# Gated mix of attention and a squared-ReLU MLP: the second chunk's q and k by seven block products

## The chip, the cores and the metric

The kernel runs on one core of a Trainium2 chip. The metric is the device time of one execution in microseconds. Beside it stands one execution that the hardware profiler recorded; every start and duration below is from that recording, counted from the start of its span.

## The reference, cut to what matters

2048 tokens of width 448 go through two branches that a gate mixes, all in fp32:

```python
qkv = x @ wqkv                      # 448 -> 3 x 448, 16 heads of 28
logits = q . k at offsets 0, 2, .., 14 back (8 keys), scaled, masked
a = (softmax(logits) @ v) @ wo
h = relu(x @ w1 + b1) ** 2          # 448 -> 1792
b = h @ w2 + b2
g = sigmoid((x * gate_w).sum(-1))
out = g * a + (1 - g) * b
```

## The kernel before

**Arithmetic.** Each fp32 operand of a matmul is cut into a high and a low part (`split_full`: ACT writes the high part at L130, DVE subtracts it at L131), and a product is made of three matmuls: high by high, high by low, low by high. PE therefore works on half arrays in pairs (`side_by_side` L194 to L202 and `beside` L349, whose matmuls are issued by `Bank.add` at L344): one product goes through the upper 64 rows of the array while another goes through the lower 64. The trace lists the two of a pair as single instructions.

**Stages.** The tokens are worked in four chunks of 512. First come q, k and v of chunk 0 (`qkv_first`), of chunk 1 (two calls of `qkv_two`, each for 256 tokens), of chunk 2 (`qkv_seven`) and of chunk 3 (`qkv_two` twice, with the first groups h of the MLP between). `qkv_seven` does q and k of two token halves by Strassen's way: seven block products (banks x, y, z, w and so on in the trace, numbered 1 to 7 in the code) in place of eight, from sums of token blocks (`token_sums`) and sums of weight blocks (`weight_sums`), which DVE makes and `split_full` cuts. Its v goes through the class `V`, without sums. After that comes the MLP, chunk by chunk (h, then b = h @ w2), and at the end a @ wo (the banks a and last). Attention runs beside this in 8 units (`par`, `g`): a unit loads q, k and v (L532, L533, L538) from DRAM, POOL multiplies (L561, L568) and DVE reduces (L562, L576).

**Where q, k and v go.** A finished PSUM bank is copied by ACT into an SBUF tile (`qkv_evacuate` L243, in `qkv_seven` `copied` L433 and `added` L437 on DVE) and stored to DRAM by SP (`stage_store` L235, into q_d, k_d and v_d). These tiles, named st in the trace, come from the pool tag "stage", which has three buffers (`ST_BUFS`) used in turn: a fourth tile can be written only when the first one's store has landed. `qkv_seven` takes the stage tile of its second token half from another tag ("e5"), and chunk 2's v goes to the tag "pp" and to two tiles of other use (`own_v`, `b2t`). A bank that PE will go on with after its copy is "turned" first (a memset of one element by DVE, L212 and L360), and the copy itself must be done before PE writes the bank again.

**Order of the work.** PE's order is that of the code. Everything else is placed by a planner's clock, in ns: `advance` adds 203 for each pair of matmuls that PE is given, and `when(t, ...)`, `steps(t, gap, ...)` and `at(dt, ...)` emit their work as the clock passes t. The trace runs 5.7 to 5.9 us behind this clock. So each engine's list, SP's DMA list too, is fixed in the program, and each engine takes its list in order: an instruction that waits holds up all behind it. The numbers that matter here are those of `SPLIT_AT` (cuts of chunk c of x, from raw tiles into the tiles x), the spill of x to DRAM (`x_spill`, L157, four stores of 512 KB into x_d for each chunk), the loads and cuts of w1 in four pieces (`w1_piece`, load at L759), and the load of w2 (`w2_piece`, load at L792 into the tile w2raw, whose four rows are cut by `split_copied`: ACT writes the high part at L745 and a copy into PSUM at L746, DVE the low part at L751).

## Time and profile before

| | us |
|---|---|
| median of 3 runs (lowest, highest) | 413.1 (412.44, 413.24) |
| the profiled execution's own time | 412.9 |
| its span | 411.1 |
| PE busy | 406.5 |
| DVE, ACT, POOL busy | 278.8, 218.0, 267.8 |
| mean granted clock of PE | 1.0 |

The span is what the core's instructions cover; the 1.8 us between it and the execution's time lie outside the program's instructions. Busy time of PE counts a matmul from its start to its modelled end, and a share near 100% means that PE had nearly always something in flight. Names in the trace drop the numbers of buffers: `st<-qkv` is a copy of some qkv bank into some stage tile.

### The profile page before, as it was taken

The numbers are of one execution on the slowest core, as the hardware profiler recorded it, in microseconds if no ns is written. First come the engines' busy times: TensorE is split into PE (matmuls) and PEld (weight loads), VectorE is DVE, ScalarE is ACT, GpSimd is POOL, SyncE is SP. The second block draws the span as 40 slices with busy tenths as digits, with TensorE's granted clock in tenths as the row PEclk, the third lists the DMA queues.
The fourth block names the chain that finished last, engine by engine and source line by source line (L and its number), as shares of the span: only waits on it lengthen the run. The fifth ranks groups of instructions, "written<-read, shape, count | busy, mean of one in ns | idle before, by whom it ended". The sixth has DMA issues, their size and how long they took to land.

```text
span 411.1 us, 9365 instructions
## 1 busy us (share of the span) xinstructions
PE 406.5 (99%) x3817; PEld 398.4 (97%) x3817; DVE 278.8 (68%) x454; ACT 218.0 (53%) x494; POOL 267.8 (65%) x167
## 2 busy tenths in 40 slices
PE   8999999999999999999999999999999999999997
PEld 7999999999999999999999999999999999999996
DVE  4575866484868667587665888788676776784344
ACT  5664777474875455445565435454653254356640
POOL 0000000966999999989898899899899797950000
PEclk9999999999999999999999999999999999999999
DMA  7999899989271514554113638875146530058404
GB/s 231 347 353 341 247 365 299 367 233 334 97 262 76 208 36 151 206 186 153 19 68 120 206 100 239 238 190 162 38 145 202 216 130 0 25 153 156 119 2 180
DMA packets 67020, 74.00 MB, mean 180 GB/s; under 512 B 33504, under 2 KB 59296, under 8 KB 66848
## 3 DMA queue, kind: packets, MB, share of 16 engines
q1 hardware_dynamic: 66976, 73.39, 56.2%
q8 instruction: 30, 0.49, 0.5%
q14 instruction: 14, 0.11, 0.1%
HBM read 45.94 MB, written 28.25 MB: 180 GB/s over the span
## 4 chain that ended last, share of the span: by engine, by line
PE 98%; DMA 1%; DVE 0%; SPq 0%; issue 0%
PE b L202 33%; PE h L202 32%; PE qkv L202 17%; PE a L202 7%; PE v L344 2%; PE qkv L291 2%; PE x L344 1%; PE z L344 1%; PE a L1273 1%; DMA xraw<-xT 1%; PE y L344 1%; PE w L344 1%; PE last L1273 0%; DVE bt L1152 0%; SPq L886 0%; PE last L1265 0%
## 5 line engine op out<-in xcount | busy, mean ns | idle before, releaser
L561 POOL TENSOR_TENSOR qk<-q,k 128x896 f32<-128x896 f32 x64 | 134.9, 2143 | 82.2 <-DMA k<-k_d 76.8
L568 POOL TENSOR_TENSOR av<-lg,v 128x896 f32<-128x896 f32 x64 | 119.2, 1970 | 5.0 <-DVE lg L562 4.8
L866 DVE TENSOR_TENSOR h<-h,h 128x512 fp32r<-128x512 f32 x56 | 38.5, 687 | 60.2 <-ACT h L869 60.1
L202 PE MATMUL b<-w2ah,h 64*128 64x448 f32 x448 | 71.9, 359 | 0.0
L202 PE MATMUL b<-w2bh,h 64*128 64x448 f32 x448 | 71.6, 359 | 0.0
L576 DVE TENSOR_REDUCE o<-av 128x112 f32<-128x896 f32 x64 | 66.6, 1070 | 0.5 <-POOL av L568 0.3
L562 DVE TENSOR_REDUCE lg<-qk 128x32 f32<-128x896 f32 x64 | 66.9, 1074 | 0.0
L867 ACT ACTIVATE h<-h,b1z 128x512 f32<-128x512 f32 x56 | 36.7, 655 | 42.4 <-PE h L202 42.4
L202 PE MATMUL qkv<-wqh,x 64*128 64x448 f32 (+1 forms) x384 | 57.4, 360 | 0.0
L202 PEld LDWEIGHTS b<-w2ah,h 64*128 64x128 f32 x448 | 50.8, 184 | 0.0
L202 PEld LDWEIGHTS b<-w2bh,h 64*128 64x128 f32 x448 | 50.5, 184 | 0.0
L202 PE MATMUL b<-w2al,h 64*128 64x448 f32 x224 | 46.8, 358 | 0.0
L202 PE MATMUL b<-w2bl,h 64*128 64x448 f32 x224 | 46.7, 358 | 0.0
L202 PEld LDWEIGHTS qkv<-wqh,x 64*128 64x128 f32 x384 | 36.5, 184 | 2.5
L202 PE MATMUL qkv<-wql,x 64*128 64x448 f32 (+1 forms) x192 | 35.2, 360 | 0.0
L868 ACT ACTIVATE h<-h 128x512 fp32r<-128x512 f32 x56 | 33.6, 599 | 1.7
L869 ACT ACTIVATE h<-h 128x512 f32<-128x512 f32 x56 | 33.2, 594 | 0.0
L814 ACT ACTIVATE h<-h 128x4 fp32r<-128x4 f32 (+1 forms) x35 | 7.2, 207 | 44.0 <-PE b L202 41.6
L202 PEld LDWEIGHTS b<-w2al,h 64*128 64x128 f32 x224 | 27.3, 184 | 0.0
L202 PEld LDWEIGHTS b<-w2bl,h 64*128 64x128 f32 x224 | 27.1, 184 | 0.0
L243 ACT ACTIVATE st<-qkv 128x448 f32<-128x448 f32 x36 | 18.1, 542 | 16.3 <-PE qkv L202 13.8
L202 PEld LDWEIGHTS qkv<-wql,x 64*128 64x128 f32 x192 | 18.4, 184 | 1.3
(263 smaller groups left out, 889.3 us busy)
## 6 DMA issues: line engine op xcount, KB each, us to landing
k<-k_d SPq DMA_DIRECT2D x8, 840.0 KB, 6.5
v<-v_d SPq DMA_DIRECT2D x8, 840.0 KB, 4.9
x_d<-x SPq DMA_DIRECT2D x12, 512.0 KB, 6.7
q_d<-st SPq DMA_DIRECT2D x8, 448.0 KB, 5.6
k_d<-st SPq DMA_DIRECT2D x8, 448.0 KB, 5.3
w1raw<-w SPq DMA_DIRECT2D x4, 896.0 KB, 10.2
q<-q_d SPq DMA_DIRECT2D x8, 448.0 KB, 3.7
o_d<-o SPq DMA_DIRECT2D x16, 224.0 KB, 2.3
```

The lines of the kernel that those rows point to most:

```text
L202: nc.tensor.matmul(acc.pt[:, :acc.n], a[rows], w[rows], start=acc.todo == acc.all, stop=acc.todo == 1)
L243: nc.scalar.activation(st[:, :, t % 2], heads(pt), AF.Copy)
L291: nc.tensor.matmul(acc.pt[:, :D], a, w, start=k == j == 0, stop=False)
L344: nc.tensor.matmul(self.pt[:, :self.n], a, w, start=new, stop=True, skip_group_check=True)
L561: nc.gpsimd.tensor_mul(pr, q[:, s:s + 1].to_broadcast([P, W, C]), k[:, s:s + W])
L562: pending.append(lambda: nc.vector.tensor_reduce(lg[:, s], pr.rearrange("p w (h d) -> p w h d", h=HG), axis=AX.X, op=ALU.add))
L568: nc.gpsimd.tensor_mul(pr.rearrange("p (h d) w -> p w h d", h=HG), lg[:, s][:, :, :, None].to_broadcast([P, W, HG, DH]), v[:, s:s + W].rea ...
L576: nc.vector.tensor_reduce(o[:, g * C:(g + 1) * C], pr, axis=AX.X, op=ALU.add)
L866: nc.vector.tensor_sub(hl, pt, f32(hh))
L867: ops += [lambda pt=pt, r=r: nc.scalar.activation(pt, pt, AF.Relu, bias=b1t[:, f + r:f + r + 1]), lambda pt=pt, hh=hh: nc.scalar.activatio ...
L868: lambda pt=pt, hh=hh: nc.scalar.activation(hh, pt, AF.Square),
L869: lambda pt=pt, r=r, low=low: (nc.scalar.activation(pt, pt, AF.Square), at(delays[r], low))]
```

## The change

`qkv_seven(1, ...)` takes the place of chunk 1's two `qkv_two`. Its v goes through `V` with stage tiles of the pool (`inner` is None). `token_sums(1)` is made on chip into tiles of x0, x1 and the attention's tag "v". The sums of the weights, and their cuts, are emitted from clock 8300 on instead of 17000. In the table, entries after chunk 1 move; the first load of w2 moves from 85500 to 87000 and its cuts stay at 93200, and the spill of chunk 2's x moves from 40000 to 71000. Attention's start moves by 2500.

```diff
-ATT_DELAY = 16000.0
+ATT_DELAY = 18500.0
...
             a, b = sums[self.c, (None, 1, 0, 0, 1)[n]], (None, 1, 0, 1, 0)[n]
-            o = (2 * self.u + b) * P if j < 2 else CH + b * P
-            return tuple(t[:, o:o + P] for t in a)
+            o = (2 * self.u + b) * P if j < 2 else b * P
+            return tuple(t[:, o:o + P] for t in a[j // 2])
...
-                if self.inner == "pp":
+                if self.inner in (None, "pp"):
                     qkv_evacuate(bank.pt, self.c, tl, 2, self.inner)
...
-    SPLIT_AT = {1: 19000.0, 2: 35000.0, 3: 53500.0}
+    SPLIT_AT = {1: 18800.0, 2: 33200.0, 3: 51700.0}
...
+        one = [lambda: sub(q0, k0, q0), lambda: sub(k0, k1, k0), lambda: sub(k1, k1, q0), lambda: sub(q1, q1, k1)]
+        two = [lambda: sub(q2, k2, q2),
+               lambda: sub(k2[LOW], o[LOW], k2[LOW]), lambda: sub(k2[HIGH], m[HIGH], k2[HIGH]),
+               lambda: sub(z[LOW], o[LOW], q2[LOW]), lambda: sub(z[HIGH], m[HIGH], q2[HIGH]),
+               lambda: sub(m[LOW], m[LOW], z[LOW]), lambda: sub(m[HIGH], o[HIGH], z[HIGH])]
+        cuts = [cut((1, False), q0), cut((3, False), k0), cut((2, False), k1), cut((4, False), q1)]
+        cuts += [lambda: split_full(o, *w7x, soon)]
+        return one, two, cuts, [cut((1, True), q2), cut((2, True), z), cut((4, True), m), cut((3, True), k2)]
...
         def begin():
+            if c == 1:
+                t = [xpool.tile([P, 2 * CH], F32R, tag=f"x{n}", name=f"s{c}_0{'hl'[n]}")[:, 48:48 + CH + 2 * P] for n in range(2)]
+                sums[c, 0] = [[v[:, :CH] for v in t], [v[:, CH:] for v in t]]
+                t = attp.tile([P, 48 + 2 * (CH + 2 * P)], F32R, tag="v", name=f"s{c}_1")[:, 48:]
+                t = [t[:, n * (CH + 2 * P):(n + 1) * (CH + 2 * P)] for n in range(2)]
+                sums[c, 1] = [[v[:, :CH] for v in t], [v[:, CH:] for v in t]]
+                return
...
-    steps(17000.0, 900.0, weight_sums())
+    one, two, cuts, more = weight_sums()
+    steps(8300.0, 700.0, one)
+    steps(13600.0, 700.0, cuts)
+    steps(16300.0, 700.0, two)
+    steps(27000.0, 0.0, more[:1])
+    steps(30500.0, 900.0, more[1:])
     for c, t in SPLIT_AT.items():
         when(t, x_begin, c)
         for k in range(4):
             when(t + k * 900.0, lambda c, k: x_split(xraw[c], xs[c], k, soon if c == 3 else now), c, k)
         if c < 3:
-            when(t + 5000.0, lambda c: x_spill(c, xs[c]), c)
+            when((0.0, 24000.0, 71000.0)[c], lambda c: x_spill(c, xs[c]), c)
     when(23500.0, x_more, 2)
     when(39500.0, x_more, 3)
 
-    def sums_begin():
-        made, cuts = token_sums(2)
-        steps(43000.0, 850.0, made)
-        steps(50300.0, 2100.0, cuts)
-    when(42500.0, sums_begin)
+    def sums_begin(c, t, gap, t_cut, gap_cut):
+        made, cuts = token_sums(c)
+        steps(t, gap, made)
+        steps(t_cut, gap_cut, cuts)
+    when(23300.0, sums_begin, 1, 23400.0, 850.0, 27500.0, 2000.0)
+    when(40900.0, sums_begin, 2, 41000.0, 850.0, 48500.0, 2100.0)
     when(10500.0, x_spill, 0, x)
-    when(25000.0, w1_piece, 0, 38000.0, 1500.0)
+    when(25000.0, w1_piece, 0, 37000.0, 1500.0)
     when(44500.0, halos)
-    when(45500.0, w1_piece, 1, 58000.0, 1300.0)
-    when(66800.0, w1_piece, 2, 76300.0, 1400.0)
-    when(67800.0, w1_piece, 3, 83500.0, 900.0)
+    when(44500.0, w1_piece, 1, 56200.0, 1300.0)
+    when(65000.0, w1_piece, 2, 74500.0, 1400.0)
+    when(66000.0, w1_piece, 3, 85000.0, 850.0)
     for j in range(2):
-        when(65500.0 + j * 2000.0, x_copy, 3, j)
-    when(78500.0, biases)
-    when(85500.0, w2_piece, 0, 4, 93200.0, 1500.0)
-    when(89100.0, w2_piece, 4, 3, 99700.0, 1400.0)
+        when(63700.0 + j * 2000.0, x_copy, 3, j)
+    when(76700.0, biases)
+    when(87000.0, w2_piece, 0, 4, 93200.0, 1500.0)
+    when(89600.0, w2_piece, 4, 3, 99700.0, 1400.0)
...
-    qkv_two(xs[1], 1, 0)
-    qkv_two(xs[1], 1, 2)
+    qkv_seven(1, xs[1], (None, None))
```

PE's chunk 1 before consists of 252 half matmuls of `side_by_side`; now it has 234 of `Bank.add`, and the rest of PE's list is as it was. In the second pass over a bank (`other`, `second`) PE waits for the ACT copy of what the first pass left there.

**ACT, the copies of chunk 1.** ACT's list before, where the first q and k banks of chunk 1 are copied into stage tiles (st1_0_0 holds q, st1_1_1 k, x2 are chunk 2's tokens):

```order
L243 ACTIVATE st1_0_0_649<-qkv1_0_0_534 128x4x112 [waits DMAHW6_49,PE_49,Activation_49]
L243 ACTIVATE st1_1_1_651<-qkv1_1_1_537 128x4x112 [waits DMAHW3_49,Activation_49]
L130 ACTIVATE tw8_208<-wqraw0_3_153 64x448 [waits DVE_49]
L130 ACTIVATE x2_0_666<-xraw2_0_487 128x512 [waits DMAHW7_49,DMAHW1_49]
L130 ACTIVATE tw8_208<-wqraw7_172 64x448 [waits DVE_49]
L130 ACTIVATE x2_1_667<-xraw2_1_488 128x512 [waits DMAHW2_49,DMAHW0_49]
L243 ACTIVATE st1_0_0_649<-qkv1_1_0_535 128x4x112 [waits PE_49]
L243 ACTIVATE st1_1_1_651<-qkv1_0_1_536 128x4x112
L130 ACTIVATE x2_2_668<-xraw2_2_489 128x512 [waits DMAHW1_49]
```

And in the change, where v, x and z are copied (st1_0_2 is v's tile of tokens 0 and 1, DMAHW is a wait on a DMA):

```order
L130 ACTIVATE tw8_208<-wqraw0_3_153 128x448
L130 ACTIVATE w2ah_74<-wqraw1_164 128x448
L433 ACTIVATE st1_0_0_660<-x1_0_584 128x4x112 [waits DVE_49,DMAHW3_49,PE_49,Activation_49]
L433 ACTIVATE st1_1_0_662<-x1_1_586 128x4x112 [waits DVE_49]
L130 ACTIVATE x2_0_673<-xraw2_0_499 128x512 [waits DMAHW7_49,DMAHW1_49]
L130 ACTIVATE x2_1_674<-xraw2_1_500 128x512 [waits DMAHW2_49,DMAHW0_49]
L130 ACTIVATE x2_2_675<-xraw2_2_501 128x512 [waits DMAHW1_49]
L130 ACTIVATE x2_3_676<-xraw2_3_502 128x512 [waits DMAHW4_49,DMAHW2_49]
L433 ACTIVATE st1_0_1_714<-z1_0_664 128x4x112 [waits DVE_49,DMAHW1_49,PE_49,Activation_49]
L433 ACTIVATE st1_1_1_716<-z1_1_666 128x4x112 [waits DMAHW2_49,DVE_49,Activation_49]
```

The cuts of x2 now stand between x's copies and z's, and each of the two z copies waits for a DMA: the first for the v_d store of st0_2_2, the second for the v_d store of st1_0_2. PE's second pass over z waits for the second of them.

**SP, behind chunk 0.** SP's list of DMAs before, from the load of the first piece of w1 (st0 are chunk 0's tiles, st1 chunk 1's):

```order
L759 DMA w1raw0_524<-w1 128x4x448 [waits DMAHW0_49]
L235 DMA v_d_59<-st0_2_2_528 128x4x224 [waits DMAHW1_49,Activation_49]
L235 DMA q_d_57<-st1_0_0_649 128x4x224 [waits DMAHW2_49,Activation_49]
L235 DMA k_d_58<-st1_1_1_651 128x4x224 [waits DMAHW3_49,Activation_49]
L235 DMA v_d_59<-st1_0_2_712 128x4x224 [waits DMAHW4_49,Activation_49]
L808 DMA xraw3_772<-xT 128x2048 [waits DMAHW5_49]
```

The same piece of SP's list in the change (halo0 are the zeros ahead of the first token):

```order
L759 DMA w1raw0_537<-w1 128x4x448 [waits DMAHW0_49]
L235 DMA v_d_59<-st0_2_2_541 128x4x224 [waits DMAHW1_49,Activation_49]
L235 DMA v_d_59<-st1_0_2_626 128x4x224 [waits DMAHW2_49,Activation_49]
L808 DMA xraw3_765<-xT 128x2048 [waits DMAHW3_49,DVE_49]
L1021 DMA k_d_58<-halo0_128 8x7x112 [waits DMAHW4_49,Pool_49]
L1021 DMA v_d_59<-halo0_128 8x7x112 [waits DMAHW5_49]
```

Now a v_d store of chunk 1 follows the v_d store of chunk 0 at once, and the q_d and k_d stores of chunk 1 come later, behind the halos and the second w1 load.

**SP, around the first w2 load.** SP's list before, from the load of the bias b2 (q01 and k01 are loads for the attention, st3 chunk 3's tiles):

```order
L1025 DMA b2t_76<-b2 128x448 [waits DMAHW5_49,DMAHW1_49]
L532 DMA q01_1430<-q_d_57 128x896 [waits DMAHW6_49,Pool_49]
L533 DMA k01_1431<-k_d_58 128x1680 [waits DMAHW7_49]
L792 DMA w2raw0_1444<-w2 128x4x448 [waits DMAHW0_49,Activation_49]
L235 DMA q_d_57<-st3_0_0_1412 128x4x224 [waits Activation_49]
L235 DMA k_d_58<-st3_1_1_1414 128x4x224 [waits DMAHW2_49,Activation_49]
L235 DMA v_d_59<-st3_0_2_1478 128x4x224 [waits DMAHW3_49,Activation_49]
L792 DMA w2raw4_1539<-w2 128x3x448 [waits DMAHW4_49,DVE_49]
```

SP's list in the change, at the same place:

```order
L1025 DMA b2t_76<-b2 128x448 [waits DMAHW5_49,DMAHW1_49]
L235 DMA q_d_57<-st3_0_0_1423 128x4x224 [waits DMAHW6_49,Activation_49]
L235 DMA k_d_58<-st3_1_1_1425 128x4x224 [waits DMAHW7_49,Activation_49]
L532 DMA q01_1472<-q_d_57 128x896 [waits DMAHW0_49,Pool_49]
L533 DMA k01_1473<-k_d_58 128x1680
L235 DMA v_d_59<-st3_0_2_1479 128x4x224 [waits DMAHW2_49,Activation_49]
L792 DMA w2raw0_1543<-w2 128x4x448 [waits DMAHW3_49]
L792 DMA w2raw4_1554<-w2 128x3x448 [waits DMAHW4_49,DVE_49]
```

The load w2raw0 stood ahead of the three stores of st3 and now stands behind them. The four x_d stores of chunk 2, which stood behind xraw3, come now between chunk 2's q_d and v_d stores.

**ACT, around the cuts of w2raw0.** In the change, where the copies of chunk 3's third q and fourth k bank stand (st3_2_0, st3_3_1):

```order
L745 ACTIVATE w2ah_74<-w2raw0_1543 128x448 [waits DMAHW3_49]
L746 ACTIVATE copy6_1491<-w2raw0_1543 128x448 [waits Activation_49]
L745 ACTIVATE w2ah_74<-w2raw0_1543 128x448
L746 ACTIVATE copy6_1491<-w2raw0_1543 128x448 [waits DVE_49]
L243 ACTIVATE st3_2_0_1615<-qkv3_2_0_1485 128x4x112 [waits DMAHW6_49,PE_49]
L243 ACTIVATE st3_3_1_1617<-qkv3_3_1_1488 128x4x112 [waits DMAHW7_49]
L745 ACTIVATE w2ah_74<-w2raw0_1543 128x448
```

Before, three pairs of cut and copy stood ahead of st3_2_0; now two pairs do. In both, PE's next h group waits for the copy into st3_2_0.

More of the change, by code (lines that the diff above doesn't have):

```diff
@@ L944, in weight_sums @@
         (q0, q1, q2, m), (k0, k1, k2) = ([t[:, :D] for t in raws[b]] for b in range(2))
-        o = raw7[:, 1, :D]
+        o, z = raw7[:, 1, :D], raw7[:, 0, :D]
         sub = nc.vector.tensor_sub
@@ L949, in cut @@
             return lambda: split_full(t, *wsum[key], soon)
[L951 to L965 removed]
+        one = [lambda: sub(q0, k0, q0), lambda: sub(k0, k1, k0), lambda: sub(k1, k1, q0), lambda: sub(q1, q1, k1)]
[6 more added lines that the diff above has]
+        return one, two, cuts, [cut((1, True), q2), cut((2, True), z), cut((4, True), m), cut((3, True), k2)]
     def token_sums(c):
[L969 removed]
+        raw = xraw[c] if isinstance(xraw[c], list) else [xraw[c][:, k, :CH] for k in range(4)]
         add, sub = nc.vector.tensor_add, nc.vector.tensor_sub
@@ L980, in begin @@
         def begin():
+            if c == 1:
[5 more added lines that the diff above has]
+                return
             for j in range(2):
-                sums[c, j] = [halfp.tile([P, FA], F32R, tag=f"e{2 * j + n}", name=f"s{c}_{j}{'hl'[n]}")[:, 48:48 + CH + 2 * P]
-                              for n in range(2)]
+                t = [halfp.tile([P, FA], F32R, tag=f"e{2 * j + n}", name=f"s{c}_{j}{'hl'[n]}")[:, 48:48 + CH + 2 * P]
+                     for n in range(2)]
+                sums[c, j] = [[v[:, :CH] for v in t], [v[:, CH:] for v in t]]
         def cut(j):
-            split_full(raw[j], *(t[:, :CH] for t in sums[c, j]), soon)
+            split_full(raw[j], *sums[c, j][0], soon)
             for u, rows in enumerate((LOW, HIGH)):
-                split_full(raw[2 + j][rows, u * 2 * P:(u + 1) * 2 * P], *(t[rows, CH:] for t in sums[c, j]), soon)
+                split_full(raw[2 + j][rows, u * 2 * P:(u + 1) * 2 * P], *(t[rows] for t in sums[c, j][1]), soon)
         return made(0) + made(2), (lambda: (begin(), cut(1)), lambda: cut(0))
```

16 lines of the change are left out of this document (removed).

## The prediction

> **What bounds the kernel.** I read the page first: span, busy shares, granted clock.
>
> ```profile
> span 411.1 us, 9365 instructions
> PE 406.5 (99%) x3817; PEld 398.4 (97%) x3817; DVE 278.8 (68%) x454; ACT 218.0 (53%) x494; POOL 267.8 (65%) x167
> PEclk9999999999999999999999999999999999999999
> ```
>
> PE works 406.5 of 411.1 us at full clock, so a change can win only by taking matmuls out, and loses whatever PE then waits. The chain that ended last gives the stages and the price of a matmul (start, length, what).
>
> ```profile
> 13.17 43.66 PE qkv L202 x432
> 56.83 2.48 PE v L344 x24
> ...
> 60.51 1.86 PE v L344 x18
> ...
> 70.18 1.20 PE z L344 x12
> ...
> 80.53 22.99 PE qkv L202 x228
> 103.52 2.84 PE h L202 x24
> ```
>
> Each row begins where the one before ends: PE never pauses here. A half-array matmul costs 43.66/432 = 0.101 us. Those 432 are chunk 0's last 180 and chunk 1's 252, so chunk 1 begins at 13.17 + 180 × 0.101 = 31.4 and takes 25.5 us. Chunk 2, already by seven products, runs from 56.83 to 80.53: 23.7 us. Of chunk 3, the first MLP group h starts at 103.52, 23.0 us after the chunk.
>
> **What is removed.** In the changed order chunk 1 has 234 half matmuls for 252; the rest of PE's order is identical. 18 × 0.101 = **−1.8 us**, and the two chunks' lengths say the same (25.5 − 23.7). That is the whole gain.
>
> **What is added beside PE.** Eight sums and their cuts go to DVE and ACT, which stand at 68% and 53%, and the weights' sums come earlier. DVE's memsets ahead of a bank's second half now come behind more work in its list; no row shows one late, so I bound them by nothing and by one such piece of work:
>
> ```profile
> 27.88 0.67 DVE L131 TENSOR_TENSOR x<-xraw,x 128x512 fp32r<-128x512 f32 x1
> ```
>
> I take nothing for them, because the wait below, later in the same chunk, swallows a delay of 0.67 us; without that wait they would count. Attention starts 2.5 us later in the planner. That costs nothing either: wo's first use waits for PE alone, not for attention's result:
>
> ```profile
> ACT oh L1222 <- PE a L202: 9.3, 4, 2.8
> ```
>
> If that cover were gone it would cost up to those 2.5 us, at the end. The remaining w1 loads and cuts mostly move 1.0 to 1.8 us earlier with PE's shorter program, so against their users they stay. The fourth w1 piece's cuts move behind chunk 3's first q and k copies:
>
> ```profile
> 90.51 1.04 ACT L130 ACTIVATE w1bh<-w1raw 128x448 fp32r<-128x448 f32 x2
> ...
> 92.31 1.25 ACT L130 ACTIVATE w17h<-w1raw 64x64 fp32r<-64x64 f32 x4
> ```
>
> These 2.3 us still fit into the time for which ACT idles ahead of the w2 cuts (4.67 us, below), so I take nothing, and 2.3 at most if that idle time were gone. What remains is where an ACT copy that PE needs now stands behind a DMA. I find two places.
>
> **First wait, in chunk 1.** The stage pool holds three buffers, so a copy into the fourth tile waits for the store of the first. Before, q, k and v of chunk 1 came out late and the stores ahead had landed. Now chunk 1's v tile of tokens 0 and 1 takes a buffer of its own, and the first z copies take the buffers of the v stores of rows 41 and 42 in SP's list. Row 41 is an instruction of before, too:
>
> ```profile
> 35.48 1.15 SPq L759 DMA_DIRECT2D w1raw<-w  x1
> 36.73 1.25 SPq L235 DMA_DIRECT2D v_d<-st  x1
> ```
>
> The DMA views of those moments give size and time to landing:
>
> ```profile
> w1raw<-w SPq DMA_DIRECT2D x1, 896.0 KB, 8.6
> v_d<-st SPq DMA_DIRECT2D x1, 448.0 KB, 8.8
> ```
>
> So it lands at 36.7 + 8.8 = 45.5. The new store of row 42 goes when both v banks are copied. In chunk 2 the v product's second part ends at 62.37, 5.5 us after the chunk's start, hence at 36.9 here, and the copies follow:
>
> ```profile
> 62.46 0.55 ACT L243 ACTIVATE st<-v 128x448 f32<-128x448 f32 x1 [0.29 <-ACT x L130]
> 67.22 0.98 ACT L433 ACTIVATE st<-z 128x448 f32<-128x448 f32 x2 [0.67 <-PE z L344]
> ```
>
> Two copies with their sums' column take about 1.1 us, so the issue is at about 38.2. What a second store lands after a first, two stores of before show, first their issues, then their views:
>
> ```profile
> 55.59 0.38 SPq L235 DMA_DIRECT2D q_d<-st  x1
> 56.09 1.13 SPq L235 DMA_DIRECT2D k_d<-st  x1
> ```
>
> ```profile
> q_d<-st SPq DMA_DIRECT2D x1, 448.0 KB, 8.9
> k_d<-st SPq DMA_DIRECT2D x1, 448.0 KB, 9.8
> ```
>
> They were issued 0.5 us apart, so they landed 1.4 apart; I take 45.5 + 1.4 = 46.9. Then one copy of 0.55 and about 0.1 of signalling: PE goes on with z at 47.6. In chunk 2 PE began that second pass over z 13.35 us after the chunk's start (70.18 − 56.83), which is 44.7 here. Wait: **+2.9 us**. Ends: both stores land together, so both copies run from 45.5 (46.6: +1.9); the store takes the 9.8 us of the k_d row from 38.2 (48.0: +4.0). Chunk 2's own such copy, whose buffers were free, waited for PE and not for a store (the row at 67.22).
>
> **Second wait, at the first MLP group.** PE's next h needs the copy of chunk 3's third q bank, which in ACT's order stands behind the cuts of the first w2 load. Before, that load left SP ahead of chunk 3's first q, k and v stores, of which the last row is the q store:
>
> ```profile
> 89.03 0.33 SPq L532 DMA_DIRECT2D q<-q_d  x1
> 89.40 0.42 SPq L533 DMA_DIRECT2D k<-k_d  x1
> 89.92 0.38 SPq L792 DMA_DIRECT2D w2raw<-w  x1
> 92.01 0.37 SPq L235 DMA_DIRECT2D q_d<-st  x1
> ```
>
> Its view from issue to landing, and ACT from there:
>
> ```profile
> w2raw<-w SPq DMA_DIRECT2D x1, 896.0 KB, 9.4
> ```
>
> ```profile
> 99.36 0.58 ACT L745 ACTIVATE w2ah<-w2raw 128x448 fp32r<-128x448 f32 x1 [4.67 <-DMA w2raw<-w]
> 99.84 0.53 ACT L746 ACTIVATE copy<-w2raw 128x448 f32<-128x448 f32 x1
> 100.31 0.56 ACT L745 ACTIVATE w2ah<-w2raw 128x448 fp32r<-128x448 f32 x1
> 101.06 0.55 ACT L746 ACTIVATE copy<-w2raw 128x448 f32<-128x448 f32 x1 [0.19 <-DVE w2al L751]
> ...
> 102.79 0.96 ACT L243 ACTIVATE st<-qkv 128x448 f32<-128x448 f32 x2
> ```
>
> ACT idled 4.67 us for the load, and the copy at 102.79 was done 0.2 us before h started. There is no slack. Now the load stands behind q_d, k_d, q, k and v_d, and the chunk-2 spill of x, four transfers of 512 KB, stands 31 us of planner time later in SP's list, behind chunk 2's q stores. The queue was then free only for a moment (start to end: sum, PE, PEld, DVE, ACT, POOL, clock, DMA share, GB/s):
>
> ```profile
> 86.00:88.00 2.00, 2.00 (x22) 1.87 (x21) 1.91 (x8) 1.20 (x4) 2.00 (x2) 1.00 0.66 163
> 88.00:90.00 2.00, 2.00 (x22) 1.87 (x22) 2.00 (x5) 1.24 (x3) 1.00 (x1) 1.00 0.19 43
> 90.00:102.00 12.00, 12.00 (x122) 11.15 (x122) 5.45 (x17) 7.04 (x19) 6.29 (x3) 1.00 1.02 334
> ```
>
> At 334 GB/s the spill's 2.1 MB take 6.3 us and the free part of 86 to 90 swallows 2.3: 4.0 us stay, and the queue is free at about chunk start + 13.5. Counted from chunk 3's start, q_d's store is issued at 92.01 − 80.53 = 11.5, and moves from about 12.2. From there to the end of the w2 load lie three stores of 448 KB, q's 448, k's 840 and w2's 896: 3.6 MB, 10.8 us at 334 GB/s. So the load lands at 23.0 with a free queue and 24.3 behind the spill; with the 354 GB/s of 20 to 31 us it would be 22.4.
>
> ```profile
> 20.00:31.00 11.00, 11.00 (x112) 10.28 (x112) 8.01 (x19) 7.23 (x17) 0.00 (x0) 1.00 1.03 354
> ```
>
> I take the middle, 23.4. Two cuts and two copies take 2.2 us (99.36 to 101.55), the bank's copy 0.55, signalling 0.1: h at 26.3 instead of 23.0, **+3.3 us** (ends 2.3 and 4.2). In the new order two pairs of cut and copy stand ahead, not three; that is counted. It comes on top of the first wait, since it is reckoned from chunk 3's own start.
>
> That adds transfers up in SP's order, as the two stores at 55.6 and the rows from 89.9 ended. One rule of the Trainium skill speaks against it: the page "DMA: Bandwidth & Descriptors", section "Queues, rings and completion order", says that completion is not first in, first out for one issuing engine. By it the w2 load might pass the stores, and the sum would be that of the first wait alone (414.0, a rival below); the trace so far agrees with the order.
>
> **Sum.** Against the profiled execution, 412.9 us (span 411.1 and 1.8 around it; the three runs' median is 413.1): 412.9 − 1.8 + 2.9 + 3.3 = **417.3 us**, with both waits at their lower ends 415.3, at their upper 419.3.
>
> **Rivals.**
> - Only the second wait (412.9 − 1.8 + 3.3 = 414.4): v_d's store of row 42 lands by 44 because the queue drains faster than the w1 load's 8.6 us suggests. Against it: row 41 alone lands at 45.5, already 0.8 after z's turn. Chance 0.14.
> - Only the first (412.9 − 1.8 + 2.9 = 414.0): w2's load passes its neighbours and lands by chunk start + 20. For it: nothing orders it behind the stores but the queue. Chance 0.10.
> - Neither (412.9 − 1.8 = 411.1, the other side, faster): ACT's copies would need both: the v store before 43.9 and the w2 load before +20. It turns on how fast the queue drains: the v store would have to take 7.2 us for 8.8, the w2 load's 3.6 MB 7.8 for 10.8, both at a rate that no window above has. What speaks for it is only that both waits are reckoned from transfers under another load than the one they will meet. Chance 0.12.
> - The clock falls in the longer pause. The profile has PE idle only ahead of chunk 0, where matmuls ran slowly:
>
> ```profile
> 1.20 3.14 PE L879 MATMUL warm<-zero 128*128 128x256 f32 x13 [1.20 <-DVE b1z L877]
> 7.81 0.96 PE L291 MATMUL qkv<-wqh,x 128*128 128x448 f32 x4
> ```
>
>  There 256 columns took 0.242 us (0.94 ns a column), later 448 took 0.24 (0.54). If a pause brought that rate back for as long as the first row, 3.1 us of work would do 1.8 us' worth: +1.3, 418.6. Before has no such pause to test it. Chance 0.08. The Trainium skill, page "TensorE: Matmul & The Clock Gate", section "Part 1: The HAM clock gate (the "warmup" mystery)", gives about 3.4 us of idleness as what sends the clock back; by it a pause of 2.9 escapes and one of 3.3 is at the edge.
> - Anything else, mostly a further wait in chunk 1 from DVE's fuller list: chance 0.06, about 418.0 with the 0.67 us on top.
>
> **How the numbers follow.** Both waits: chance 0.50, 417.3. The range runs from 413.0, so that both one-wait cases lie in it, to 419.5, for both upper ends and the clock: it leaves out the case with neither wait and part of the rest. What measurement can tell from no change is 0.2%, 0.8 us. Faster by more (below 412.3): the neither case and a little, 0.13. Within: 0.07, from one-wait cases at half size. Slower: 0.80. The case of a loss has a range of its own of 415 to 419.5.
>
> **What would show it.** Chunk 1's PE rows should number 234 and end near 57.9 with a pause of about 3 us before a z row, ended by ACT's copy, and ACT idle there by a v_d store. The h row after chunk 3 should start about 26 us after the chunk, with ACT's first w2 cut, ended by w2raw, about 23.4 us after it (18.8 in the table above). Chunk 1 with no pause, or w2raw landed before chunk 3's start + 20, would make the sum wrong; so would a pause of PE at a memset in chunk 1.

## The result, and the profile after

The changed kernel takes 423.9 us (median of 4 runs, 423.4 to 425.6) against 412.8 of the kernel before in the same session: ratio 1.0276, 95% interval 1.0245 to 1.0307. That is slower by 11 us, where I forecast 4.4. The profiled execution took 423.4. Single runs of one kernel spread by 1 to 4 us in most of the experiments below, and each session has its own runs of before; differences of less than a microsecond between two kernels are read from the interval, or not at all.

The page of the changed kernel:

```profile
span 421.4 us, 9370 instructions
PE 408.7 (97%) x3799; PEld 363.9 (86%) x3799; DVE 287.7 (68%) x480; ACT 218.4 (52%) x498; POOL 268.4 (64%) x167
PEclk9999999999699999999999999999999999999999
```

18 matmuls fewer, as said, but PE's share fell to 97%, and one slice of the granted clock shows a 6. The waits view, PE's own rows (us in total, times, longest):

```profile
PE h L202 <- ACT st L243: 6.1, 1, 6.1
PE z L344 <- DVE z L360: 0.7, 1, 0.7
PE z L344 <- ACT st L433: 0.6, 1, 0.6
```

The kernel before has none of these three rows. Since PE's order is the same from chunk 2 on, the same PE instruction can be looked up in both traces, and the difference of its starts tells where the time went:

| the same PE instruction | before, us | after, us | later by |
|---|---|---|---|
| beginning of chunk 2 | 56.88 | 57.23 | 0.4 |
| beginning of chunk 3 | 80.58 | 81.66 | 1.1 |
| first h, ahead of the pause | 103.36 | 104.44 | 1.1 |
| first h, behind the pause | 103.82 | 111.52 | 7.7 |
| end of the first h group | 106.12 | 114.89 | 8.8 |
| a later h group | 113.35 | 122.70 | 9.4 |
| first groups b | 120.72 | 130.55 | 9.8 |
| MLP, second chunk | 247.88 | 258.07 | 10.2 |

So the 1.8 us that chunk 1 wins are lost by its end, with 0.4 more; 0.7 us go in chunk 2; 6.6 us at one place, ahead of h; 1.1 right behind it; 1.5 in small pieces later.

**Chunk 0.** PE begins the half-array matmuls of chunk 0 0.3 us earlier than in the profile of before, and begins chunk 1 0.3 us later (31.48 for 31.22). The waits view lists nothing there, because PE still had matmuls in flight. Two of DVE's turns (L212) now stand behind the new sums and their cuts, the first of them here:

```profile
26.75 0.61 DVE L954 TENSOR_TENSOR wqraw<-wqraw,wqraw 64x448 f32<-64x448 f32 x1
27.36 0.06 DVE L212 MEMSET qkv<- 1x1 f32 x2
```

Behind it PE starts a pair of matmuls at 27.50, 0.38 after the pair ahead, and the next one 0.31 later, where pairs otherwise start 0.20 apart; at 29.56 the same happens again. Together they cost 0.6 us, and every profile of the seven products loses that much or more there (0.6 to 1.1 us).

**Chunk 1.** Two pauses, in PE's timeline (start, length, what, idle time before and its releaser):

```profile
40.97 0.37 PE L344 MATMUL y<-wqh,x 64*128 64x448 f32 x2
42.03 0.47 PE L344 MATMUL z<-w2ah,s 64*128 64x448 f32 x2 [0.69 <-DVE z L360]
...
45.57 0.37 PE L344 MATMUL x<-w2ah,s_0l 64*128 64x448 f32 x2
46.55 0.47 PE L344 MATMUL z<-wqh,x 64*128 64x448 f32 x2 [0.61 <-ACT st L433]
```

Pairs otherwise start 0.20 apart; here they start 1.06 and 0.98 apart, so the pauses cost 0.86 and 0.78, and about 0.1 each in the pair behind. The chain of waits names the second:

```profile
38.23 7.62 DMA v_d<-st
...
45.95 0.55 ACT st L433
...
46.55 1.48 PE z L344 x12
```

This is the store that the prediction named, issued when it said (38.2), landed at 45.9 instead of 46.9. In chunk 2 another 0.7 us go: an ACT copy waits for chunk 1's q stores, and the cuts of chunk 2's sums stand behind it.

**Ahead of h.** SP's timeline, then ACT's:

```profile
94.29 0.38 SPq L235 DMA_DIRECT2D q_d<-st  x1
94.75 0.46 SPq L235 DMA_DIRECT2D k_d<-st  x1
95.31 0.86 SPq L532 DMA_DIRECT2D q<-q_d  x1
96.22 1.18 SPq L533 DMA_DIRECT2D k<-k_d  x1
97.49 0.45 SPq L235 DMA_DIRECT2D v_d<-st  x1
97.99 2.58 SPq L792 DMA_DIRECT2D w2raw<-w  x2
```

```profile
93.28 1.42 ACT L243 ACTIVATE st<-qkv 128x448 f32<-128x448 f32 x3 [2.01 <-DMA k_d<-st]
...
108.15 0.58 ACT L745 ACTIVATE w2ah<-w2raw 128x448 fp32r<-128x448 f32 x1 [9.96 <-DMA w2raw<-w]
108.63 0.53 ACT L746 ACTIVATE copy<-w2raw 128x448 f32<-128x448 f32 x1
109.10 0.56 ACT L745 ACTIVATE w2ah<-w2raw 128x448 fp32r<-128x448 f32 x1
109.85 0.55 ACT L746 ACTIVATE copy<-w2raw 128x448 f32<-128x448 f32 x1 [0.19 <-DVE w2al L751]
110.33 0.96 ACT L243 ACTIVATE st<-qkv 128x448 f32<-128x448 f32 x2
```

The q store left 12.7 us after chunk 3's start (81.6), not 11.5: the copy ahead of it waited 2.01 us for a stage buffer, that is for chunk 2's k store, which stood behind the moved spill of x. From there the order is as forecast; the load landed 26.5 us after the chunk's start, ACT idled 9.96 us for it, and h went on at 110.9. The granted clock meanwhile (start to end: sum, then busy time and count of PE, PEld, DVE, ACT, POOL, then clock, DMA share, GB/s):

```profile
104.00:106.00 2.00, 0.83 (x7) 0.40 (x5) 0.00 (x0) 0.00 (x0) 1.47 (x1) 1.00 1.06 401
106.00:108.00 2.00, 0.00 (x0) 0.00 (x0) 0.00 (x0) 0.00 (x0) 2.00 (x2) 0.75 1.04 374
108.00:110.00 2.00, 0.00 (x0) 0.00 (x0) 0.81 (x2) 1.66 (x4) 2.00 (x2) 0.50 0.09 33
110.00:112.00 2.00, 1.09 (x6) 0.90 (x8) 2.00 (x3) 2.00 (x5) 1.79 (x3) 0.50 0.02 4
112.00:114.00 2.00, 2.00 (x14) 1.58 (x12) 1.39 (x3) 1.23 (x3) 2.00 (x2) 0.55 0.00 0
114.00:116.00 2.00, 2.00 (x22) 1.82 (x20) 2.00 (x3) 0.31 (x2) 1.68 (x1) 1.00 0.00 0
```

PE resumes at half clock and does 14 matmuls in a window that holds 22 afterwards.

### The profile page after: what moved, and what is told of

Its sections match the earlier page's. It is cut to its first block, busy times and chain, and to the rows that moved or that the text cites. A ratio compares the mean times of both kernels' runs of the same rounds, so it can differ in the third digit from the quotient of the medians.

```text
span 421.4 us, 9370 instructions
## 1 busy us (share of the span) xinstructions
PE 408.7 (97%) x3799; PEld 363.9 (86%) x3799; DVE 287.7 (68%) x480; ACT 218.4 (52%) x498; POOL 268.4 (64%) x167
## 4 chain that ended last, share of the span: by engine, by line
PE 82%; DMA 8%; ACT 4%; DVE 4%; issue 1%; SPq 0%; ACTq 0%
PE b L202 31%; PE h L202 29%; PE a L202 7%; PE qkv L202 5%; PE v L344 3%; DMA w2raw<-w 2%; DMA v_d<-st 2%; PE x L344 2%; DMA q_d<-st 1%; PE z L344 1%; PE qkv L291 1%; DMA xraw<-xT 1%; DMA k_d<-st 1%; ACT st L243 1%; DVE lg L562 1%
## 5 line engine op out<-in xcount | busy, mean ns | idle before, releaser
L202 PEld LDWEIGHTS b<-w2ah,h 64*128 64x128 f32 x448 | 41.7, 184 | 4.7 <-DVE h L866 0.9
L202 PEld LDWEIGHTS b<-w2bh,h 64*128 64x128 f32 x448 | 42.1, 184 | 3.6
L202 PE MATMUL b<-w2bl,h 64*128 64x448 f32 x224 | 40.6, 358 | 0.0
L202 PE MATMUL b<-w2al,h 64*128 64x448 f32 x224 | 40.5, 358 | 0.0
L202 PE MATMUL qkv<-wqh,x 64*128 64x448 f32 (+1 forms) x240 | 37.1, 362 | 0.0
L814 ACT ACTIVATE h<-h 128x4 fp32r<-128x4 f32 (+1 forms) x35 | 7.2, 207 | 44.4 <-PE b L202 44.3
L202 PEld LDWEIGHTS qkv<-wqh,x 64*128 64x128 f32 x240 | 24.1, 184 | 2.1 <-DVE qkv L212 0.6
L202 PE MATMUL qkv<-wql,x 64*128 64x448 f32 (+1 forms) x120 | 23.1, 360 | 0.0
L202 PEld LDWEIGHTS b<-w2al,h 64*128 64x128 f32 x224 | 21.0, 184 | 2.0
L202 PE MATMUL h<-x,w1ah 64*128 64x512 f32 x84 | 18.4, 405 | 0.2 <-ACT w1ah L814 0.2
L243 ACT ACTIVATE st<-qkv 128x448 f32<-128x448 f32 x24 | 12.1, 545 | 11.2 <-PE qkv L202 8.1
```

What stands on the lines that cost most here:

```text
L202: nc.tensor.matmul(acc.pt[:, :acc.n], a[rows], w[rows], start=acc.todo == acc.all, stop=acc.todo == 1)
L243: nc.scalar.activation(st[:, :, t % 2], heads(pt), AF.Copy)
L814: nc.scalar.activation(ap, f32(ap), AF.Copy)
```

## The experiments

Theory after the result: the place of the first w2 load in SP's list makes the pause ahead of h, and the pause makes the slow clock. Rivals: the late spill of x; attention's delay; chunk 1's own lateness. All diffs are against the change unless said otherwise. Lists of runs that build on one another give only what each adds.

### The load alone

```diff
-    when(87000.0, w2_piece, 0, 4, 93200.0, 1500.0)
+    when(83700.0, w2_piece, 0, 4, 93200.0, 1500.0)
```

> The change with one number altered: the first w2 load at clock 83700 instead of 87000, so that it leaves SP ahead of chunk 3's first q and k stores. Theory (the position of that load costs nearly all of the loss): it leaves at about 92.4 us, lands by about 98, ACT does not wait for it, PE's 6.1 us pause ahead of h and the slow clock behind it (1.4 us) go: about 415.0 us. Rival (the late spill of x holds the queue and is the cause): the load still lands late, above 103 us, and the time stays above 419.

418.2 us, ratio 1.0129 (1.0112 to 1.0146). The load left at 92.06 and landed at 99.00; the pause at that place and the slow clock are gone. But 3.2 us more than I expected remain, and most of them are a wait that the first had hidden. PE's waits view, POOL's, DVE's and ACT's timeline of this run:

```profile
PE h L202 <- ACT w1ah L814: 3.3, 2, 1.9
```

```profile
105.67 6.24 POOL L561 TENSOR_TENSOR qk<-q,k 128x896 f32<-128x896 f32 x3 [14.90 <-DMA k<-k_d]
```

```profile
103.00 0.61 DVE L751 TENSOR_TENSOR w2al<-copy,w2ah 128x448 fp32r<-128x448 f32 x1
107.83 1.09 DVE L562 TENSOR_REDUCE lg<-qk 128x32 f32<-128x896 f32 x1 [4.21 <-POOL qk L561]
108.83 0.61 DVE L751 TENSOR_TENSOR w2al<-copy,w2ah 128x448 fp32r<-128x448 f32 x1
```

```profile
109.48 0.55 ACT L746 ACTIVATE copy<-w2raw 128x448 f32<-128x448 f32 x1 [3.93 <-DVE w2al L751]
109.96 0.19 ACT L814 ACTIVATE w1ah<-w1ah 128x2 fp32r<-128x2 f32 x1
```

Read from the top: the second unit's k lands late, so POOL's product comes late, DVE's reduce of it stands at the head of DVE's list and waits 4.2 us, the low part of w2 waits behind it, ACT's next copy into the same PSUM bank behind that, and the small copy at L814 (128x2), for which PE's second h waits, behind that. An engine off PE's path reached it through two in-order lists.

### The spill alone, and both

```diff
-            when((0.0, 24000.0, 71000.0)[c], lambda c: x_spill(c, xs[c]), c)
+            when((0.0, 24000.0, 38200.0)[c], lambda c: x_spill(c, xs[c]), c)
```

> The change with one number altered: chunk 2's x is spilled at clock 38200, near its place before, instead of 71000. Theory (the load's position): the queue is free sooner but the load still stands behind five transfers, q's store leaves about 1.7 us earlier against chunk 3's start, the pause ahead of h shrinks from 6.1 to about 2.5 us and the clock stays up: about 418. Rival (the spill is the cause): no pause ahead of h, about 415.

423.2 us, ratio 1.0233 (1.0206 to 1.0260): neither theory nor rival. In the profiled run, the longest of the four (425.7), the pause ahead of h shrank only to 5.0 us, and a pause of 2.2 appeared in chunk 1, where the v store landed at 47.6, with the spill's stores issued behind it from 41.5 on. That these delayed it is not shown: in the next run they stand in the same place, and the store landed at 45.6. The slow clock came in chunk 1 as well (PE's waits, then windows with the columns as above):

```profile
PE h L202 <- ACT st L243: 5.0, 1, 5.0
PE z L344 <- ACT st L433: 2.2, 1, 2.2
```

```profile
46.00:48.00 2.00, 0.10 (x2) 0.00 (x0) 0.00 (x0) 0.28 (x1) 0.00 (x0) 1.00 1.01 406
48.00:50.00 2.00, 1.68 (x10) 1.52 (x12) 0.62 (x1) 2.00 (x6) 0.00 (x0) 0.53 1.04 424
50.00:52.00 2.00, 2.00 (x16) 1.81 (x14) 0.98 (x5) 1.58 (x6) 0.00 (x0) 0.62 1.05 434
```

With load and spill both moved:

> Both numbers altered, load at 83700 and spill at 38200. Theory: as with the load alone, about 415, since nothing of the pause was left there. Rival (each takes part of it away): one or more us below the better of the two single alterations.

416.0 us, ratio 1.0069 (1.0040 to 1.0098), 2.2 below the load alone. The rival held: the late spill has a part of its own, since without it k of the second unit lands at 102.6 instead of 105.5 and the wait for w1ah falls from 3.3 to 1.1 us.

### The kernel before, with late load and late spill

Against the kernel before:

```diff
-    when(85500.0, w2_piece, 0, 4, 93200.0, 1500.0)
+    when(88800.0, w2_piece, 0, 4, 93200.0, 1500.0)
-            when(t + 5000.0, lambda c: x_spill(c, xs[c]), c)
+            when((0.0, 24000.0, 72800.0)[c], lambda c: x_spill(c, xs[c]), c)
```

> The kernel before, chunk 1 by two calls of qkv_two as it was, with only the two table entries of the change: the w2 load at 88800 and the spill of chunk 2's x at 72800 (each 1800 later than in the change, because this chunk 1 is that much longer). Theory: the pause ahead of h has nothing to do with the seven products, so it appears here too, with 5 to 6 us and a slower clock behind it: 419 to 421. Rival (it needs chunk 1's lateness from the seven products): within 2 us of before, below 415.

The four runs fall apart: 422.0, 429.2, 430.6 and 430.7, so no ratio is given; three lie far above the 419 to 421 that I expected. The profiled one (430.7) has the pause ahead of h, 6.5 us, and a second of 4.5 in chunk 2, which is taken up under the runs with three moves. The run of 422.0 has no profile. That made this kernel a poor test, and the load was put late alone, again against the kernel before:

```diff
-    when(85500.0, w2_piece, 0, 4, 93200.0, 1500.0)
+    when(88800.0, w2_piece, 0, 4, 93200.0, 1500.0)
```

> The kernel before with one number altered: the first w2 load at 88800 instead of 85500, behind chunk 3's q and k stores and the second unit's loads. Theory (its place is the cause by itself): it lands about 24 us after chunk 3's start, PE pauses 3 to 4 us ahead of h, the clock falls behind it, 417 to 418.5. Rival (it takes the late spill or the seven products as well): within 1 us of before.

419.8 us, ratio 1.0160 (1.0144 to 1.0176), a little more than I expected. One number in the old kernel gives 7 us: 5.1 in the pause and 2.0 behind it at half clock, by the same table of starts.

```profile
PE h L202 <- ACT st L243: 4.6, 1, 4.6
```

The theory stands: the place of that load needs neither the seven products nor the spill.

### Does the pause slow the clock?

```diff
+        if c == ORDER[0] and f == 0:
+            for _ in range(24):
+                nc.tensor.matmul(accs[0].pt[:, :CH], x.h[0][:, :P], x.h[1], start=True, stop=True)
         go([h_last(x, a, f) + h_full(x, a, f + r, (0, 1, 2)) for r, a in enumerate(accs)], MM512)
```

> The change with 24 matmuls of 512 columns put ahead of the first h group, into its own bank, which the group then starts anew; they add no result and fill PE's pause of 6.1 us. Theory (the pause itself lowers PE's clock): h starts when it did, at about 110.9 us, but at full clock, and 1.4 us are won: 422.5. Rival (the slow rows behind the pause are something else than the clock): nothing won, 423.9 or more.

422.0 us, ratio 1.0221 (1.0184 to 1.0257), against 1.0276 of the change. PE's h goes on at 111.0 (110.9 in the change), but the clock stays:

```profile
110.00:112.00 2.00, 2.00 (x13) 1.46 (x13) 2.00 (x3) 2.00 (x5) 1.91 (x3) 1.00 0.01 4
112.00:114.00 2.00, 2.00 (x20) 1.67 (x20) 1.39 (x3) 1.34 (x3) 2.00 (x2) 1.00 0.03 8
```

At the end of the first h group this run is 7.5 us behind the kernel before, the change 8.8: the clock's part is 1.2 us. Shown.

### Taking the moves back

Load at 83700 and attention's delay as before:

```diff
-ATT_DELAY = 18500.0
+ATT_DELAY = 16000.0
```

> The change with the w2 load at 83700, as in the run before, and attention's delay back at 16000, so that the second unit's q and k loads leave SP ahead of chunk 3's stores. Theory (what was left with the load alone, 418.2, is DVE standing at a reduce for POOL, which waits for that unit's k; behind it DVE's low parts of w2, behind them ACT, behind ACT the row that PE's h waits for, 3.3 us): k lands some 5 us sooner, the two waits of h for w1ah go, 415. Rival (the loads only change places, the w2 load is then late again): the pause moves back to the copy of the q bank, 417 or more.

417.5 us, ratio 1.0121 (1.0081 to 1.0161). k landed 4 us sooner (101.4), the waits for w1ah shrank to 0.2, but the w2 load landed at 103.7 behind it and the pause at the q bank's copy was back with 1.8 us: the rival. In these two runs with the late spill, only one of the two loads landed in time.

All three moves back (83700, 16000, spill at 38200):

> The change with all three moves taken back (w2 load 83700, attention's delay 16000, spill of chunk 2's x at 38200); only chunk 1 and the smaller shifts stay changed. Theory (all loss behind chunk 2 comes from these three): nothing waits at h, 0.3 us behind before at chunk 2's end, 413.5. Rival (the spill between chunk 1's transfers delays the v store that chunk 1's z copies wait for): PE waits 2 us or more in chunk 1, 415 or above.

417.1 us, ratio 1.0096 (1.0067 to 1.0124): the rival again, 1.8 us at chunk 1's z, and a new wait of 1.2 us for a DVE turn in chunk 3. DVE's rows there, of this run and then of the change, are the same instructions:

```profile
97.24 2.56 DVE L131 TENSOR_TENSOR w1bl<-w1raw,w1bh 128x448 fp32r<-128x448 f32 x1 [0.81 <-ACT w1bh L130]
99.72 3.10 DVE L131 TENSOR_TENSOR w17l<-w1raw,w17h 64x64 fp32r<-64x64 f32 x4
```

```profile
97.11 0.63 DVE L131 TENSOR_TENSOR w1bl<-w1raw,w1bh 128x448 fp32r<-128x448 f32 x1 [0.76 <-ACT w1bh L130]
97.65 1.17 DVE L131 TENSOR_TENSOR w17l<-w1raw,w17h 64x64 fp32r<-64x64 f32 x4
```

Four times and nearly three times as long, and what differs is POOL, which multiplies in this run from 97.20 on:

```profile
97.20 4.59 POOL L561 TENSOR_TENSOR qk<-q,k 128x896 f32<-128x896 f32 x2 [6.14 <-DMA k<-k_d]
```

The 4.5 us pause in the profiled run of the kernel before with late load and late spill, one of the three long ones, looks the same. POOL's and DVE's rows of that run, then the row of the same cuts in the kernel before:

```profile
68.36 8.90 POOL L561 TENSOR_TENSOR qk<-q,k 128x896 f32<-128x896 f32 x4 [66.97 <-DMA k<-k_d]
```

```profile
71.26 6.46 DVE L131 TENSOR_TENSOR w17l<-w1raw,w17h 64x64 fp32r<-64x64 f32 x4
77.72 0.06 DVE L360 MEMSET w<- 1x1 f32 x2
```

```profile
69.01 1.18 DVE L131 TENSOR_TENSOR w17l<-w1raw,w17h 64x64 fp32r<-64x64 f32 x4
```

Its first k landed 4 us earlier than before (68.2), so POOL ran beside DVE's low parts of w1, and the turn of w, for which PE waited, stood behind them.

Chunk 2's x cut as before, its spill behind the load of chunk 3's x:

```diff
-    SPLIT_AT = {1: 18800.0, 2: 33200.0, 3: 51700.0}
+    SPLIT_AT = {1: 18800.0, 2: 35000.0, 3: 51700.0}
-            when((0.0, 24000.0, 38200.0)[c], lambda c: x_spill(c, xs[c]), c)
+            when((0.0, 24000.0, 42500.0)[c], lambda c: x_spill(c, xs[c]), c)
```

> The same with chunk 2's x cut at 35000 as before, not at 33200, and its spill at 42500, behind the load of chunk 3's x. Theory (DVE's and ACT's cuts of x2 stand ahead of the z turns and copies of chunk 1): the 0.7 us wait for DVE's turn of z goes, the wait for the v_d store stays or grows by as much, as PE comes to it sooner: 412.5 to 413.5. Rival (the v_d store takes all of it): no better than the run with the three moves alone.

421.8 us, ratio 1.0218 (1.0185 to 1.0252), worse than the theory and the rival. The z turn's wait went, and one of 4.6 us for the x turn came, with half clock behind it: two cuts of x2 now stood in ACT's list behind the z copies, these behind the v store, and DVE's x turn behind the cuts. So the landing of that store reached PE here too, by way of ACT's and DVE's lists.

### Chunk 1's store, and the rest

Load at 83700, spill at 43000, attention's delay most of the way back, at 17000, and:

```diff
-    when(66000.0, w1_piece, 3, 85000.0, 850.0)
+    when(66000.0, w1_piece, 3, 81700.0, 900.0)
```

> The change with all moves behind chunk 2 taken back: w2 load 83700, spill of chunk 2's x at 43000 (behind the load of chunk 3's x), the fourth w1 piece's cuts at 81700 with 900 between them, attention's delay 17000. Theory (in the run with three moves taken back DVE's low parts of that piece took 2.6 us instead of 0.6 while POOL multiplied, and DVE's turns came late behind them): these cuts are done before POOL's second unit begins, no wait of 1.2 us in chunk 3, the lag at h is that of chunk 1 and 2 alone: about 415. Rival (the reduces, not the cuts, hold the turns): a wait of PE's qkv rows for DVE of about 1 us stays, 416 to 417.

415.3 us, ratio 1.0059 (1.0030 to 1.0088); no wait in chunk 3, as the theory said. To it is added:

```diff
-    when(25000.0, w1_piece, 0, 37000.0, 1500.0)
+    when(33500.0, w1_piece, 0, 37000.0, 1500.0)
```

> As the run before in this list, and the first w1 load at 33500, behind the two v stores that chunk 1's z copies wait for, not at 25000 ahead of them. Theory (the first wait is the landing of these stores, queued behind the w1 load's 896 KB): they land 2.4 us sooner, at about 42.5 and 43.5, no z row waits for ACT, 0.6 to 1.8 us better than the run before, about 414. Rival (that wait is ACT's own work on x2, not the store): the wait stays.

414.2 us, ratio 1.0032 (1.0016 to 1.0049). No z row waits for ACT any more, where it was 1.6 us in the run before: the first wait is the store's landing behind the w1 load. The 0.7 us for DVE's turn of z in chunk 1 stay, and some of the first wait reappears in chunk 2:

```profile
PE x L344 <- DVE x L360: 0.8, 1, 0.8
```

Two variants of this kernel did not move it. Chunk 2's x cut at 35000:

> As the run before in this list, and chunk 2's x cut at 35000 instead of 33200. Theory: DVE's turn of z comes ahead of the x2 lows (no 0.7 us wait), and since the z copies no longer hold ACT, the 4.6 us wait for the x turn that the earlier run with this number had is gone too: 0.7 us better, 413.3. Rival (ACT's list is simply too full there): that x turn is late again, 415 or more.

414.2 us, 1.0023 (1.0003 to 1.0043), between theory and rival: the z turn's wait went and one of 0.4 for w came. Attention's delay at 16000:

> The run with the w1 load at 33500, and attention's delay 16000, as before the change, in place of 17000. Theory (k of the first unit lands some 2 us later than before, because this chunk 1 gives its stores at its end, so DVE's reduces placed for 16000 hold DVE's turns in chunk 2): a wait of 0.7 us or more for an x turn in chunk 2, 0.5 to 1 slower than the run with 17000. Rival (the delay is not needed): the same or faster, since the second unit's loads leave 1 us sooner.

414.0 us, 1.0021 (1.0002 to 1.0039): not slower, so the longer delay is not needed here; the rival.

From that last one on, both w2 pieces wholly back against PE's program:

```diff
-    when(87000.0, w2_piece, 0, 4, 93200.0, 1500.0)
-    when(89600.0, w2_piece, 4, 3, 99700.0, 1400.0)
+    when(83700.0, w2_piece, 0, 4, 91400.0, 1500.0)
+    when(87300.0, w2_piece, 4, 3, 97900.0, 1400.0)
```

> The run with the w1 load at 33500 and attention's delay 16000, and the two w2 pieces wholly where they were against PE: loads at 83700 and 87300, cuts at 91400 and 97900. Everything behind chunk 2 now stands as before the change. Theory (the last 0.4 us at the second h group come from ACT's cuts of w2 standing 1.8 us too late): no wait of h for w1ah, about 413.5. Rival (it is DVE's and POOL's order of the second attention unit): 414.0, as without.

413.8 us, 1.0018 (1.0003 to 1.0033). The wait for w1ah is gone; the 0.2 us between the medians is too little to tell theory from rival. On top of it x2 cut at 35000, then, in a run of its own, at 34100:

> As the run before in this list, and chunk 2's x cut at 35000 instead of 33200. Theory (then nothing is left but the 18 matmuls and some 0.4 us of turns): 0.7 us better than the run before, 412.5 to 412.9, at or just below the kernel before. Rival (DVE's list in chunk 1 is full, a turn that is spared comes late elsewhere, as the 0.4 us wait for w showed): no better than the run before.

> As the first of this list, with chunk 2's x cut at 34100, one step later than in the change. Theory: one x2 low less ahead of DVE's turn of z, that wait 0 to 0.3 us instead of 0.7, and no other turn late: between the two runs before, 412.8 to 413.2. Rival: the x turn is late by as much.

With 35000: 414.5 us, 1.0035 (1.0020 to 1.0050), no better: the rival. With 34100: 412.9 us, 1.0004 (0.9988 to 1.0019), level with the kernel before. PE's waits view of the latter lists, behind the start, two waits of 0.2 us for DVE's turns.

So seven products for chunk 1 are to be had without a loss that these runs resolve, with this table, the best of several. Where the 1.8 us go can be read from its profile by starts of the same PE instruction. PE begins the half-array matmuls of chunk 0 0.5 us ahead of before, a lead that runs from 0.1 to 0.7 us in the profiles of the seven products; whether the change has a part in it is open. It loses 0.6 at two late turns in chunk 0, wins only 1.0 of the 1.8 in chunk 1 because of two more, and loses 0.7 at two in chunk 2; 0.3 of lead are left at chunk 3's start (80.30 for 80.58). So six late turns of DVE take back about what the 18 matmuls give, although behind the start the view lists no wait above 0.2 us. No version here beats the kernel before.

## Why the prediction was wrong

**The gain** was right: 18 matmuls, 1.8 us. It can be seen at chunk 2's start: with one DVE wait of 0.85 left in chunk 1 (the run at 413.8), PE is there 0.9 us ahead of before, having begun chunk 1 level with it.

**DVE's turns**, for which I took nothing, were the term without a reason that held. In chunk 1 the idle time ahead of z's turn, 0.69 us, is about my bound of 0.67 for one piece of work, and the store's wait shrank by it, as I had said; both together cost 1.8 us. But I had looked at chunk 1 alone: late turns cost 0.6 us more in chunk 0 and 0.7 in chunk 2, where no such wait stands behind them.

**The first wait** was right in its mechanism and mis-sized: forecast +2.9 (1.9 to 4.0), measured 0.9, because the store landed 1.0 us sooner than I had it (45.9 for 46.9) and PE came some 1.1 later (45.8 for 44.7). Moving the w1 load away removed it. Its size varies: 0.3 to 2.2 us in the profiles of the kernels that keep it, and 0.5 to 1.5 in four whose programs are the same up to there. That PE begins chunk 3 1.1 us late, as the sum has it (−1.8 + 2.9), is luck: a small first wait and late turns in three chunks add up to it.

**The second wait** was right in place, order and cause, and this is the step that did most to make the number wrong: forecast +3.3 (2.3 to 4.2), measured 6.6. Of the 3.3 missing, 1.2 are the start: I took q_d's issue from before, 11.5 after the chunk's start, and did not ask what that store's own copy waits for. It waits for a stage buffer, and the spill that I had counted in the queue delays the store that frees it. In the run with the spill alone moved back near its old place, the store leaves 11.5 after the chunk's start again. The rest is the way from the q store's issue to the load's landing, 13.8 us where I had 11.9; in that run it is 13.9, so the spill is not its cause. The DMA rates of the windows in between add up to 4.3 MB, not to the 3.6 that I counted. The missing 0.7 MB are those of the second w2 load, issued 0.9 us behind the first. In the same run, whose trace has both landings (110.0 and 111.7), the queue moved only 18 GB/s from 110 to 112 us, less than 0.1 MB, so the second load's bytes had gone before the first one's landing; in the change it likewise falls to 33 GB/s behind that landing.

**The slow clock** I had as a rival with chance 0.08 and +1.3 us. It came, at 1.2 us by the run without the pause. With the second wait sized rightly it would have been part of the forecast: I let it hang on an edge near 3.3 us, and a pause of 2.2 us was enough in the run with the spill alone.

**Attention's later start**, which I took to cost nothing, did cost, in a hidden way. I looked only at attention's end. Its second unit reaches PE at once, through DVE's list: 3.3 us in the run with the load alone, unseen in the change itself because the longer pause stands ahead. Moving attention's delay back took this wait away (0.2 us left) in the two runs made for it, but another wait came in its place (1.8 and 1.2 us), and no run shows it to save more than 0.7 us.

**The small pieces** behind the first h group, 1.5 us, I had not looked for. The run with both w2 pieces moved back has none of the first 1.0; it differs from the change in other numbers too, so what caused them stays open.

The rule of the Trainium skill, page "DMA: Bandwidth & Descriptors", section "Queues, rings and completion order", that I weighed (no order of completion) did not decide: the load landed last of its row, as it was issued (105.8 for the v store ahead of it, 108.1 for the load), and the transfers that SP issued, where the trace has their landings, landed in the order of issue in all 18 profiles.

## What to carry to other kernels

Ask of each issue time taken from an old trace what the instruction waits for in the new order: a store that moves is late by its own copy's buffer before the queue makes it late. On in-order lists, follow a late transfer through every engine that reads it, also those far off the bounding path, because one reduce that waits at the head of DVE's list held PE. Compare the starts of the same PE instruction in both traces: late turns of a few tenths each, which the waits view lists in part or not at all, took back a gain of 1.8 us. And price a pause of the matmul engine with the clock behind it: here half clock followed every pause of 2.2 us and more, and cost 1.2 to 2.3 us.

## What the runs showed of the hardware

**The granted clock changes at steps of 3.41 us, so the place of a pause decides.** Read in windows of 0.1 us and by the share of the clock in each, it stood at 0.50 from 106.99 to 113.82 us in the change, from 106.28 to 113.10 in the kernel before with the load late, and from 48.13 to 51.54 and 112.98 to 116.39 in the run with the spill alone. These are stretches of one or two times 3.41 us, and the last two begin 19 times 3.41 us apart. Cut into steps of that length from there, the three traces show what was needed: the clock fell at the end of steps in which PE had stood idle for 2.0, 2.2, 2.6 and 3.2 us, and did not in the run with the load alone, with 1.8 us (steps counted from the first rise of its clock, at 4.3). In the run with the spill alone the pause of 5.0 us ahead of h began at 107.8, with only 1.8 us of it in its first step. So the clock stayed at 1.00 until the pause was over, and fell 0.2 us after PE had resumed at 112.8:

```profile
110.00:112.00 2.00, 0.00 (x0) 0.00 (x0) 0.94 (x2) 1.79 (x4) 2.00 (x2) 1.00 0.05 18
112.00:114.00 2.00, 1.22 (x6) 1.03 (x8) 2.00 (x3) 2.00 (x6) 1.81 (x3) 0.74 0.02 4
```

The pause of 2.2 us in chunk 1 of the same run lay nearly whole in one step (46.1 to 48.1) and was enough. The price is the time that PE works before the clock returns: 2.9 us at half clock cost 1.2 in the change, 3.4 us cost 1.5 here, 4.9 us cost 2.0 in the kernel before with the load late, and 5.3 us about 2.3 in the run with the 4.6 us wait for the x turn. The Trainium skill, page "TensorE: Matmul & The Clock Gate", section "Part 1: The HAM clock gate (the "warmup" mystery)", puts the idle window at about 3.4 us and has it free-running. The steps agree with both; but a window did not have to be idle throughout, since 2.0 of its 3.4 us were enough here, and on that the measurement decides.

**A DVE subtraction is held up by POOL's products.** A DVE subtraction with both inputs in SBUF took 2.56 us for 0.63 while POOL multiplied, four small ones 6.46 for the 1.18 of before. Subtractions of the form that reads a copy in PSUM (L751) stayed at 0.6 beside the same products. The Trainium skill, page "SBUF — State Buffer", section "Who interferes with whom", has it so for a DVE instruction with two SBUF inputs against a GpSimd one that reads SBUF; the rows agree. Before, subtractions of the first form (L131) ran only while POOL stood idle (its first product begins at 72.26, its second unit at 94.95), so its profile could not show it.
